# Attention, routed experts and a dense layer: masks and tails of two heads in one product, idle products in the drain, and where the low parts of the last routing are made

## The chip, the cores and the metric

One Trainium2 chip, one core. The metric is the time of one execution on the device in microseconds (us); lower is better. TensorE is called PE, its weight loads PEld, VectorE DVE, ScalarE ACT, GpSimd POOL, SyncE SP.

## The reference

Three layers, the output of each the input of the next, all in float32:

```python
# 1. attention: 4 batches x 8 heads, 576 tokens, head size 64
scores = q @ k.T / 8 ; bias = -(cum_i - cum_j), cum = cumsum(max(s, 0))
scores = where(j > i, -1e9, scores + minimum(bias, 0))
x = softmax(scores) @ v                       # as 2304 tokens x 512
# 2. experts: 8 experts of 512 -> 1024 -> 512, each token goes to one
e = argmax(x @ w_gate) ; g = softmax(x @ w_gate)[e]
x = g * (relu(x @ w1[e]) @ w2[e])
# 3. dense: 512 -> 2048 -> 512
h = relu(x @ w_in) ; out = (h * h) @ w_out
```

To keep float32 precision most operands are cut into a high part (a rounded copy, made by ACT) and a low part (what is left, a subtraction on DVE or POOL), and a product is made as high by high, high by low and low by high.

## The kernel before, in words

**Order of the work.** Attention and the first routing are not written in order. Each step is added to a planner (`Steps`, lines 31 to 150) with a key, the engines that may do it, a cost for each of them in ns, the steps it needs (`need`), the buffers it uses (`use`) and a due time. `Steps.run` (lines 67 to 150) is a list schedule made when the kernel is built: of the steps that could start within 60 ns of the earliest on an engine it takes the one due first, holding up to 200 ns (`HOLD`) for one due over 100000 ns (`URGENT`) earlier; due times are passed back to what a step needs (lines 68 to 70). Each engine then runs its instructions in that order, whatever they take on the chip. The experts and the dense layer (`Moe.run`, lines 1548 to 1631) are written out by hand.

**Attention** (lines 153 to 745). Work goes by head n = 0 to 31, in units of four heads; tails go by pairs. A sequence of 576 is four blocks of 128 and a tail of 64. `maxima` (521 to 608) makes a row maximum for the softmax: products into PSUM tiles `mx` (lines 536 and 539), DVE reductions (561, 581), and a DMA of the result back into the operand `qB` (607). `scores` (632 to 670) makes the scores transposed: `score` (622 to 630) is a product with `kA,qA` (626), one with `kB,qB` (627) and, on the diagonal, one with a mask (629). Each head has three pieces of 512 columns in tiles `tt` (piece 0 holds the four diagonal blocks), each pair one tail piece in tile `ot`: both heads' 64x64 corners, one on partitions 0 to 63, the other on 64 to 127. `expo` (672 to 688) takes a piece through exp on ACT (`P`, 679), a high part on ACT (`H`, 681) and a low part (`L`, 682) on POOL or DVE, as the planner likes. `pv` (690 to 745) multiplies with v (713): for the tail rows the 64x64 corners `H_t`, `L_t` use half of the array's rows. The result is scaled into `xb` (740 on DVE, 743 on ACT).

**Routing** (`gate`, 799 to 930) runs once a batch: transposes, logits (875), a chain of small DVE operations (906 to 927) with a product on PE in its middle (`rk`, 883 to 886), and POOL's indirect DMAs into the token table (894).

**The drain** (`Moe.first`, 1155 to 1326) is what lies between the last scores and the first expert product. It makes the first expert's input in four PSUM banks (`put_in`, 1217 to 1221, its products all have line 1220): tokens of earlier batches are gathered (1125), cut in high and low (`xgh` 1240, `xgl` 1242) and multiplied by unit blocks (`xgt`); those of the last batch are cut (`bh` 1268, `bl` 1272) and picked by 0/1 matrices `ones` (`at`, 1281; products `take`), which need the last routing's slots (926). Then ACT and DVE cut the banks (1299, 1302) and, after a branch (1450), the experts begin (1418 to 1420). PE, ACT, DVE and POOL have this in one queue each, in order.

The lines that the change touches, of those:

```python
self.mQt, self.mTt                                   # 64x64 masks, 249 to 250
for o in range(2): mm(ps[64*o:64*o+64, 0:64], h + o, 512, 64, 512, 64)   # t2, 555
if key[0] < self.NH - self.LDVE: ...                 # 685, LDVE = 32: never true
st.add(("xgl", c), {"Pool": 1120, "DVE": 600}, ..., due=soon)    # 1242
st.add(("bl", c), {"DVE": 800, "Pool": 1430}, low, ..., due=due) # 1277
```

Of the kernel before, what the change touches and what calls it, by code (L numbers as in the profile page):

```python
# [30 lines left out]
class Steps:  # L31
# [10 lines left out]
    URGENT = 100000  # L42

    def __init__(self, bufs):
        self.bufs, self.ops, self.by, self.users = bufs, [], {}, {}
        self.groups, self.after = [], {}
# [20 lines left out]
    def run(self):  # L67
        for op in reversed(self.ops):
            for p in op["need"]:
                p["due"] = min(p["due"], op["due"] - p["ns"] - 145)  # L70
        for op in self.ops:
            op["left"], op["next"] = len(op["need"]), []
# [31 lines left out]
        while ready:  # L104
# [15 lines left out]
            t, _, e, op = min(first, key=lambda x: x[:2])  # L120
            for u in op["use"]:
# [16 lines left out]
            ready.remove(op)  # L138
            for q in op["next"]:
# [13 lines left out]
class Attention:  # L153
# [86 lines left out]
    def setup(self, moe_constants):  # L240
# [8 lines left out]
        self.mQ, self.mQt = tile("mQ", [128, 128], BF16), tile("mQt", [64, 64], BF16)  # L249
        self.mT, self.mTt = tile("mT", [128, 128], BF16), tile("mTt", [64, 64], BF16)  # L250
# [24 lines left out]
        def mQ():  # L275
            nc.gpsimd.memset(self.mQ, 0.0)
            block(self.mQ, [[-1, 128]], 0, 1)
            nc.gpsimd.memset(self.mQt, 0.0)
            block(self.mQt, [[-1, 64]], 0, 1)
# [5 lines left out]
        def mTt():  # L285
            nc.gpsimd.memset(self.mTt, 0.0)
            block(self.mTt, [[1, 64]], 0, -1)
# [10 lines left out]

        self.gps("ident16", 560, lambda: nc.gpsimd.tensor_copy(out=self.ident16, in_=self.identb), need=["identb"])
# [221 lines left out]
    def maxima(self, n):  # L521
# [12 lines left out]
        def mm(out, h, i0, M, j0, N):  # L534
# [3 lines left out]
            if j0 + N > i0:  # L538
                nc.tensor.matmul(out=out[:, N - M:], lhsT=self.identb[0:M, 0:M], rhs=self.mQ if M == 128 else self.mQt,  # L539
                                 start=False, stop=True)  # L540
# [13 lines left out]
        def t2(ps):  # L554
            for o in range(2):
                mm(ps[64 * o:64 * o + 64, 0:64], h + o, 512, 64, 512, 64)

        def red(ps, *cols):

            for c, w, at, k in cols:  # L560
# [7 lines left out]
                 ("t2", 0, 240, t2, 70, ((0, 64, 17, 1),))]  # L568
# [53 lines left out]
    def score(self, u, ps, h, j0, M, i0, N, mask=False):  # L622
# [3 lines left out]
        nc.tensor.matmul(out=ps, lhsT=kA[:, j], rhs=qA[:, i], start=True, stop=False)  # L626
        nc.tensor.matmul(out=ps, lhsT=kB[:, j], rhs=qB[:, i], start=False, stop=not mask)  # L627
        if mask:
            nc.tensor.matmul(out=ps, lhsT=self.identb[0:M, 0:M], rhs=self.mT if N == 128 else self.mTt,  # L629
                             start=False, stop=True)  # L630

    def scores(self, n):
# [8 lines left out]
        def piece(p, ps):  # L641
            if p == 0:
# [1041 lines left out]
```

## Time and profile before

| | |
|---|---|
| median of 3 runs (lowest to highest) | 922.13 us (920.59 to 922.86) |
| the profiled execution, its own time | 922.22 us |
| its span in the trace | 920.7 us |
| busy: PE, PEld, DVE, ACT, POOL | 855.1, 728.7, 660.8, 494.9, 316.1 us |
| mean granted clock of TensorE | 0.967 |

A row of the timeline has the start, the duration, the engine, the line, the operation, what it writes and reads, the shapes and a count, and in brackets how long the engine was idle before and what ended that. Rows that lie close together are merged into one with a count. A PE duration holds the way through the array, so products overlap: what a product costs the stream is the distance from its start to the next start. The windows view has, for each stretch, its length, each engine's busy time with the number of instructions, the granted clock of TensorE (1.00 is 2.4 GHz, 0.50 is 1.2 GHz), the share of the DMA engines, and GB/s. Attention takes the first 230 us, the drain goes to 261 us, the experts to about 503 us, and the dense layer takes the rest.

### The profile page before, as it was taken

Reading aid. Unit: us, or ns where it says so; the run is one execution under the profiler, and the core shown is the slowest. Engines: PE = TensorE matmul, PEld = TensorE weight load, DVE = VectorE, ACT = ScalarE, POOL = GpSimd, SP = SyncE. Lnnn points to the kernel's source line nnn. Section 1 sums busy time; section 2 is a strip of 40 time slices with the busy share of each in tenths; the row PEclk is TensorE's granted clock in tenths of the full one; section 3 lists DMA queues with packets and bytes.
Section 4 is the critical chain, followed back from the end, with each engine's and each line's share of the span. In section 5 each row is a group of like instructions: output and inputs, shape, how many; then the busy total and the mean of one; then the engine's idle time right before and its main releaser. Section 6 shows DMA issues by size and latency. Waiting matters only on the chain.

```text
span 920.7 us, 17377 instructions
## 1 busy us (share of the span) xinstructions
PE 855.1 (93%) x6582; PEld 728.7 (79%) x6582; DVE 660.8 (72%) x1211; ACT 494.9 (54%) x1009; POOL 316.1 (34%) x356
## 2 busy tenths in 40 slices
PE   3889887889799999999999999999999999999995
PEld 2677665668689999998999777888888888888894
DVE  8699989888837798889889885554455445444673
ACT  3777776878434455545556444444454445444563
POOL 6667656756613355546433450020001001000100
PEclk9999997889679999999999999999999999999998
DMA  4886974980456666786664300010001000000100
GB/s 113 155 165 152 185 137 110 180 174 3 155 169 189 237 185 192 232 265 204 210 202 140 115 0 1 1 46 1 0 1 46 1 0 15 33 1 1 46 2 23
DMA packets 155489, 94.03 MB, mean 102 GB/s; under 512 B 115292, under 2 KB 140342, under 8 KB 155402
## 3 DMA queue, kind: packets, MB, share of 16 engines
q1 hardware_dynamic: 146766, 78.82, 32.7%
q0 software_dynamic: 4096, 10.19, 3.3%
q10 hardware_dynamic: 4540, 3.87, 1.4%
q8 instruction: 53, 0.87, 0.4%
q14 instruction: 34, 0.28, 0.1%
HBM read 70.16 MB, written 10.02 MB: 87 GB/s over the span
## 4 chain that ended last, share of the span: by engine, by line
PE 59%; issue 6%; DVE 5%; ACT 1%; POOL 0%; POOLq 0%; DVEq 0%; ACTq 0%
PE y_d L1500 7%; PE hd L1420 7%; PE hd L1419 7%; PE hd L1418 7%; PE y_d L1498 7%; PE y_d L1499 6%; PE y_e L1438 3%; PE y_e L1439 3%; PE y_e L1437 3%; PE he L1418 3%; PE he L1419 3%; PE he L1420 3%; DVE wae_6l L1348 1%; DVE wbe_6l L1348 1%; DVE wbe_7l L1348 1%
## 5 line engine op out<-in xcount | busy, mean ns | idle before, releaser
L1543 POOL DMA_INDIRECT out_dram<-o,ids x18 | 18.5, 1026 | 342.0 <-ACT o L1540 339.1
L1486 DVE TENSOR_TENSOR sqd<-hd,rld 128x512 f32<-128x512 f32 (+1 forms) x80 | 50.9, 637 | 112.5 <-ACT rld L1484 111.1
L1484 ACT ACTIVATE rld<-hd 128x512 f32<-128x512 f32 (+1 forms) x80 | 44.5, 556 | 130.5 <-PE hd L1420 130.5
L682 POOL TENSOR_TENSOR L<-P,H 128x512 f16<-128x512 f32 x58 | 71.0, 1231 | 59.1 <-ACT H L681 49.2
L1490 DVE TENSOR_TENSOR ald<-sqd,ahd 128x512 fp32r<-128x512 f32 (+1 forms) x80 | 51.1, 639 | 51.6 <-ACT ahd L1489 51.6
L1489 ACT CAST ahd<-sqd 128x512 fp32r<-128x512 f32 (+1 forms) x80 | 46.3, 579 | 74.1 <-DVE sqd L1486 74.1
L1400 POOL TENSOR_TENSOR lf<-lf,pw 128x512 f32<-128x512 f32 x32 | 50.0, 1564 | 74.6 <-DVE pw L1399 56.2
L713 PE MATMUL pv<-v,H 128*128 128x65 f16 (+1 forms) x896 | 59.1, 199 | 6.7 <-DVE xb L740 5.1
L679 ACT ACTIVATE P<-tt 128x512 f32<-128x512 f32 x96 | 55.3, 594 | 16.3 <-PE tt L629 8.8
L1427 ACT ACTIVATE hhe<-he 128x400 fp32r<-128x400 f32 (+7 forms) x64 | 27.9, 437 | 64.8 <-PE he L1420 60.9
L713 PE MATMUL pv<-v,L 128*128 128x65 f16 x448 | 54.8, 197 | 7.6 <-DVE L L682 7.6
L626 PE MATMUL tt<-qA,kA 128*128 128x128 f16 (+3 forms) x352 | 57.5, 232 | 3.8 <-ACT P L679 3.8
L627 PE MATMUL tt<-qB,kB 128*128 128x128 f16 (+3 forms) x352 | 60.7, 232 | 0.0
L713 PEld LDWEIGHTS <-H 128*128 128x128 f16 x896 | 48.5, 100 | 14.7 <-issue 7.3
L681 ACT CAST H<-P 128x512 f16<-128x512 f32 x96 | 57.0, 618 | 1.1 <-ACT P L679 1.0
L1125 POOL DMA_INDIRECT xg<-x_dram,idt x20 | 21.3, 1063 | 86.6 <-PE xps L1135 68.7
L713 PEld LDWEIGHTS <-L 128*128 128x128 f16 x448 | 43.9, 103 | 8.3 <-DVE L L682 8.1
L561 DVE TENSOR_REDUCE tops<-mxb 128x1 f32<-128x128 f32 (+2 forms) x96 | 43.6, 501 | 8.2 <-PE mxb L539 8.1
L682 DVE TENSOR_TENSOR L<-P,H 128x512 f16<-128x512 f32 x38 | 39.4, 1042 | 5.1 <-ACT H L681 4.4
L1428 DVE SCALAR_TENSOR_TENSOR hle<-he,hhe 128x400 fp32r<-128x400 f32 (+7 forms) x64 | 30.7, 480 | 16.7 <-ACT hhe L1427 16.4
L626 PEld LDWEIGHTS <-kA 128*128 128x128 f16 (+1 forms) x384 | 35.3, 102 | 7.9 <-issue 3.2
L627 PEld LDWEIGHTS <-kB 128*128 128x128 f16 (+1 forms) x384 | 34.4, 103 | 5.4 <-issue 4.1
(700 smaller groups left out, 3097.2 us busy)
## 6 DMA issues: line engine op xcount, KB each, us to landing
w0s<-in_moe_w_dram SPq DMA_DIRECT2D x30, 512.0 KB
w1s<-in_moe_w_dram SPq DMA_DIRECT2D x30, 512.0 KB
wout<-in_moe_w_in_dram SPq DMA_DIRECT2D x16, 512.0 KB
wout<-in_moe_w_out_dram SPq DMA_DIRECT2D x12, 512.0 KB
ldq<-in_q_dram SPq DMA_DIRECT2D x32, 128.0 KB
ldk<-in_k_dram SPq DMA_DIRECT2D x30, 128.0 KB
ldv<-in_v_dram SPq DMA_DIRECT2D x30, 128.0 KB
x_dram<-xb SPq DMA_DIRECT2D x3, 1024.0 KB
```

The lines of the kernel that those rows point to most:

```text
L626: nc.tensor.matmul(out=ps, lhsT=kA[:, j], rhs=qA[:, i], start=True, stop=False)
L627: nc.tensor.matmul(out=ps, lhsT=kB[:, j], rhs=qB[:, i], start=False, stop=not mask)
L679: self.act(("P",) + key, w, lambda: nc.scalar.activation(out=P(), in_=ps(), func=AF.Exp, scale=0.125), need=[T], use=[use, ("P", key), ("H ...
L681: self.st.add(("H",) + key, {"ACT": 0.833 * w + 80}, lambda: nc.scalar.copy(out=H(), in_=P()), need=[("P",) + key], use=[("P", key), ("H", ...
L682: f = lambda e="Pool": (nc.gpsimd if e == "Pool" else nc.vector).tensor_tensor(out=L(), in0=P(), in1=H(), op=ALU.subtract)
L713: nc.tensor.matmul(out=ps[0:M, I, 0:N], lhsT=a, rhs=m, start=(i == 0), stop=(i == len(ops) - 1))
L1418: nc.tensor.matmul(out=ps, lhsT=wh[:, k, :], rhs=xh[:, k, 0:C], start=(k == 0), stop=False)
L1419: nc.tensor.matmul(out=ps, lhsT=wh[:, k, :], rhs=xl[:, k, 0:C], start=False, stop=False)
L1420: nc.tensor.matmul(out=ps, lhsT=wl[:, k, :], rhs=xh[:, k, 0:C], start=False, stop=(k == 3))
L1498: nc.tensor.matmul(out=acc[t], lhsT=ah[:, c], rhs=wh, start=first, stop=False)
L1499: nc.tensor.matmul(out=acc[t], lhsT=ah[:, c], rhs=wl, start=False, stop=False)
L1500: nc.tensor.matmul(out=acc[t], lhsT=al[:, c], rhs=wh, start=False, stop=last)
```

## The change

1. **Masks**: the mask of the four diagonal blocks is one product of 512 columns, ahead of the eight score products, instead of four of 128 behind them.
2. **Tails**: the tail masks become 128x128 with two blocks; the tail of a pair is one 128x128 block whose off-diagonal quarters are masked, in `maxima` (t2, reduced over 128 columns instead of 64) and in `scores` (exp, high and low parts over 128 columns instead of 64). `pv` reads 128 rows of it.
3. **Low parts**: those of heads 30 and 31, all `xgl` and all `bl` (now in two steps) are on DVE alone.
4. **Idle products**: once the planner has placed the last score piece, and sees PE idle for over 250 ns, it puts in products of the identity with zeros for 0.8 of that gap: into unused columns of a `pv` bank in use, or into a free `o` or `mx` bank.

```diff
 # Steps
+    GAP = 250
+    PART = 0.8
 # in run(), where the next op is chosen; self.keep holds the score steps not yet placed
+            gap = t - free[e] if e == "PE" and self.fill and not any(self.keep) else 0
+            if gap > self.GAP:
+                tags, width, f, tag, w2, f2 = self.fill
+                live = [k for k in order.get(tag, [])[-2:] if left[k] > 2 and isinstance(k[1], int)]
+                i = int(self.PART * gap / w2)
+                if live and i:
+                    f2(*live[-1], i)
+                    tags = ()
+                for tag in tags:
+                    o, b = order.get(tag, []), self.bufs[tag]
+                    if len(o) >= b and not left[o[-b]]:
+                        s = max(free[e], freed[o[-b]])
+                        i = int(self.PART * (t - s) / width)
+                        if i > 0:
+                            k = (tag, ("fill", n))
+                            f(*k, i)
...
 # setup
-            block(self.mQt, [[-1, 64]], 0, 1)
+            block(self.mQt, [[-1, 128]], 0, 1)
+            block(self.mQt[64:128], [[1, 128]], -64, 0)
...
-            block(self.mTt, [[1, 64]], 0, -1)
+            block(self.mTt, [[1, 128]], 0, -1)
+            block(self.mTt[0:64], [[-1, 128]], 63, 0)
+        def fill(tag, key, n):
+            out = self.tile(tag, key, [128, 512], F32)[:, 0:256]
+            for _ in range(n):
+                nc.tensor.matmul(out=out, lhsT=self.identb, rhs=self.mrow.bitcast(BF16)[:, 0:256], start=True, stop=True)
+        def fill_pv(tag, key, n):
+            for _ in range(n):
+                nc.tensor.matmul(out=self.tile(tag, key)[:, 328:512], lhsT=self.identb,
+                                 rhs=self.mrow.bitcast(BF16)[:, 0:184], start=True, stop=True)
+        self.st.fill = ("o", "mx"), 110, fill, "pv", 80, fill_pv
 # maxima
         def t2(ps):
-            for o in range(2):
-                mm(ps[64 * o:64 * o + 64, 0:64], h + o, 512, 64, 512, 64)
+            mm(ps[:, 0:128], h, 512, 128, 512, 128)
...
-                 ("t2", 0, 240, t2, 70, ((0, 64, 17, 1),))]
+                 ("t2", 0, 256, t2, 128, ((0, 128, 17, 1),))]
 # scores
             if p == 0:
+                self.nc.tensor.matmul(out=ps, lhsT=self.identb, rhs=self.mT.unsqueeze(1).to_broadcast([128, 4, 128]),
+                                      start=True, stop=False)
                 for J in range(4):
-                    self.score(u, ps[:, 128 * J:128 * J + 128], h, 128 * J, 128, 128 * J, 128, True)
+                    self.score(u, ps[:, 128 * J:128 * J + 128], h, 128 * J, 128, 128 * J, 128, on=True, more=J < 3)
...
-                for o in range(2):
-                    self.score(u, ps()[64 * o:64 * o + 64, :], h + o, 512, 64, 512, 64, True)
+                self.score(u, ps(), h, 512, 128, 512, 128, True)
...
-            self.expo((n, "t"), 64, ps, ("o", ("t", n)))
+            self.expo((n, "t"), 128, ps, ("o", ("t", n)))
 # expo
-        if key[0] < self.NH - self.LDVE:
+        if key[0] > self.NH - 3:
+            self.dve(("L",) + key, 1.04 * w, lambda: f("DVE"), **kw)
+        elif key[0] < self.NH - self.LDVE:
 # pv
-                    key, c = (n - n % 2, "t"), 0
-                    r, M = slice(64 * (h % 2), 64 * (h % 2) + 64), 64
-                    v = vt()[r, blk + 8, :]
+                    key, c = (n - n % 2, "t"), 64 * (h % 2)
+                    r, M, v = slice(0, 128), 128 - c, vt()[:, blk + 8, :]
 # Moe.first
-            st.add(("xgl", c), {"Pool": 1120, "DVE": 600}, lambda e, ...
-                use=[ug] + u, due=soon)
+            at.dve(("xgl", c), 560, lambda ...
+                use=[ug] + u, due=due)
...
-            st.add(("bl", c), {"DVE": 800, "Pool": 1430}, low, need=[("bh", c)], ..., due=due)
+            for i, n in ((0, 560), (1, 170)):
+                at.dve(("bl", c, i), n, lambda i=i, low=low: low(i), need=[("bh", c)], ..., due=due)
```

## Rows read from the trace of the kernel before

**Rows 1.** Windows: attention after its start, its end, the drain in two parts.

```profile
40.00:232.00 192.00, 165.93 (x2754) 131.63 (x2753) 170.63 (x396) 148.65 (x360) 128.10 (x143) 0.93 0.68 137
...
200.00:230.00 30.00, 29.18 (x577) 24.75 (x574) 24.85 (x69) 24.90 (x62) 19.03 (x24) 1.00 0.14 22
230.00:246.00 16.00, 10.49 (x134) 8.78 (x135) 14.31 (x37) 9.35 (x30) 10.80 (x12) 0.79 0.27 78
246.00:256.00 10.00, 10.00 (x60) 9.86 (x57) 5.68 (x28) 1.23 (x2) 5.91 (x10) 0.50 0.73 239
```

**Rows 2.** Waits of DVE for PE, 40 to 232 us: first and last of seven (total, times, longest).

```profile
DVE tops L561 <- PE mxb L539: 4.7, 5, 1.8
...
DVE g_s L889 <- PE ork L886: 0.3, 1, 0.3
```

**Rows 3.** Timeline of PE: one pair's tail scores, then the tail maxima.

```profile
110.58 0.22 PE L626 MATMUL ot<-qA,kA 128*64 128x64 f16 x1
...
111.22 0.43 PE L536 MATMUL mxt<-kB,qB 128*64 128x512 f16 x3
111.59 0.21 PE L539 MATMUL mxt<-mQt,identb 64*64 64x64 bf16 x1
...
112.02 0.23 PE L626 MATMUL tt<-qA,kA 128*128 128x128 f16 x1
```

**Rows 4.** Timeline of PE: the tail corner within one head's `pv`.

```profile
104.98 0.19 PE L713 MATMUL pv<-v,L 128*128 128x65 f16 x1
105.10 0.25 PE L713 MATMUL pv<-v,H_t 64*64 64x65 f16 x2
...
105.31 0.24 PE L713 MATMUL pv<-v,H 128*128 128x65 f16 x2
```

**Rows 5.** Groups by line and shape: the tail's reduction (busy us, mean ns, idle before).

```profile
L561 DVE TENSOR_REDUCE tops<-mxt 128x1 f32<-128x64 f32 x16 | 3.5, 216 | 2.5 <-PE mxt L539 2.2
```

**Rows 6.** Groups by line and shape: a tail mask's making, before 40 us.

```profile
L268 POOL TENSOR_SCALAR_AFFINE_SELECT mQt<-mQt 64x64 bf16<-64x64 bf16 x1 | 0.3, 332 | 0.1
```

**Rows 7.** Timeline of the drain: PE at the last pair's tail.

```profile
231.01 0.21 PE L713 MATMUL pv<-v,L_t 64*64 64x65 f16 x1 [1.44 <-POOL L_t L682]
```

**Rows 8.** Timeline of the drain: DVE, from a last low part to the 0/1 matrices.

```profile
228.62 2.17 DVE L682 TENSOR_TENSOR L<-P,H 128x512 f16<-128x512 f32 x1 [0.57 <-ACT H L681]
...
239.65 1.35 DVE L1272 TENSOR_TENSOR hlb<-xb,hhb 64x128 fp32r<-64x128 f32 x1
...
242.05 1.14 DVE L909 TENSOR_TENSOR g_sel<-g_lg,g_mx 128x40 f32<-128x40 f32 x1
...
244.41 1.26 DVE L914 TENSOR_TENSOR g_oh<-g_sel,g_smx 128x40 bf16<-128x40 f32 x1
...
247.31 1.40 DVE L1281 TENSOR_SCALAR Pones<-xbg,g_slot 128x256 fp32r<-128x256 f32 x5
```

**Rows 9.** Timeline of the drain: POOL, one of its last low parts.

```profile
239.33 1.52 POOL L1272 TENSOR_TENSOR xlb<-xb,xhb 128x512 fp32r<-128x512 f32 x1 [0.47 <-ACT xhb L1268]
```

**Rows 10.** Timeline of the drain: PE, products of line 1220 and the first expert product.

```profile
242.15 0.28 PE L1220 MATMUL pvacc<-s4aux,alx 128*128 128x128 f32 x1
242.26 0.27 PE L1220 MATMUL pvacc<-s4aux,ahx 128*128 128x128 f32 x1
...
250.77 0.41 PE L1220 MATMUL ttacc<-Pones,xlb 128*128 128x256 f32 x1
250.98 0.41 PE L1220 MATMUL ttacc<-Pones,xhb 128*128 128x256 f32 x1
...
259.04 0.28 PE L1220 MATMUL pvacc<-Pones,hlb 64*128 64x256 f32 x1
261.29 0.67 PE L1418 MATMUL he<-xhf,ahw 128*128 128x400 f32 x1 [1.98 <-DVEq L1450]
```

**Rows 11.** Timeline of PE: idle products at the kernel's start.

```profile
22.88 1.37 PE L295 MATMUL oidle<-mrow,identb 128*128 128x256 bf16 x11
```

**Rows 12.** Low parts of line 682 on DVE: ns min/median/max, first and last start.

```profile
L682 DVE TENSOR_TENSOR L<-P,H x38: 643/688/6493, 32.8 to 228.6; 128x512 f16<-128x512 f32 x38
```

More of the change, by code (lines that the diff above doesn't have):

```diff
@@ L42 @@
     URGENT = 100000
+    GAP = 250
+    PART = 0.8
     def __init__(self, bufs):
-        self.bufs, self.ops, self.by, self.users = bufs, [], {}, {}
-        self.groups, self.after = [], {}
+        self.bufs, self.ops, self.by, self.users, self.fill = bufs, [], {}, {}, None
+        self.groups, self.after, self.keep = [], {}, []
     def group(self, old, new, f):
@@ L70, in run @@
                 p["due"] = min(p["due"], op["due"] - p["ns"] - 145)
+        self.keep = [op["key"] for op in self.ops if op["key"][0] == "T"]
         for op in self.ops:
@@ L138, in run @@
             ready.remove(op)
+            if op["key"][0] == "T":
+                self.keep.pop()
             for q in op["next"]:
@@ L538, in mm @@
             if j0 + N > i0:
-                nc.tensor.matmul(out=out[:, N - M:], lhsT=self.identb[0:M, 0:M], rhs=self.mQ if M == 128 else self.mQt,
-                                 start=False, stop=True)
+                nc.tensor.matmul(out=out[:, N - M:], lhsT=self.identb, rhs=self.mQt if i0 == 512 else self.mQ, start=False, stop=True)
         def b1(o, ps):
@@ L620, in seg, with score @@
         return (2, 128 * I - 128) if J == 1 else (2, 384)
-    def score(self, u, ps, h, j0, M, i0, N, mask=False):
+    def score(self, u, ps, h, j0, M, i0, N, mask=False, on=False, more=False):
         nc = self.nc
@@ L625, in score @@
         j, i = self.cols(h, j0, M), self.cols(h, i0, N)
-        nc.tensor.matmul(out=ps, lhsT=kA[:, j], rhs=qA[:, i], start=True, stop=False)
-        nc.tensor.matmul(out=ps, lhsT=kB[:, j], rhs=qB[:, i], start=False, stop=not mask)
+        nc.tensor.matmul(out=ps, lhsT=kA[:, j], rhs=qA[:, i], start=not on, stop=False)
+        nc.tensor.matmul(out=ps, lhsT=kB[:, j], rhs=qB[:, i], start=False, stop=not (mask or more))
         if mask:
-            nc.tensor.matmul(out=ps, lhsT=self.identb[0:M, 0:M], rhs=self.mT if N == 128 else self.mTt,
-                             start=False, stop=True)
+            nc.tensor.matmul(out=ps, lhsT=self.identb, rhs=self.mTt if i0 == 512 else self.mT, start=False, stop=True)
     def scores(self, n):
@@ L1268, in high, with low @@
                     nc.scalar.copy(out=o, in_=i)
-            def low(e, rows=rows, src=src):
-                for o, i, h in zip(rows("l"), src(), rows("h")):
-                    (V if e == "DVE" else nc.gpsimd).tensor_tensor(out=o, in0=i, in1=h.bitcast(F32), op=ALU.subtract)
+            def low(i, rows=rows, src=src):
+                V.tensor_tensor(out=rows("l")[i], in0=src()[i], in1=rows("h")[i].bitcast(F32), op=ALU.subtract)
             norms = [("norm", at.H * b + 2 * c + i) for i in range(2)]
@@ L1276, in first @@
             at.act(("bh", c), 780, high, need=norms, use=ub)
-            st.add(("bl", c), {"DVE": 800, "Pool": 1430}, low, need=[("bh", c)], use=ub + [("xl", "b"), ("hl", "b")], due=due)
+            for i, n in ((0, 560), (1, 170)):
+                at.dve(("bl", c, i), n, lambda i=i, low=low: low(i), need=[("bh", c)], use=ub + [("xl", "b"), ("hl", "b")], due=due)
         ones = lambda t: at.tile("P", ("ones", t), [128, 512], F32R)[:, LO:C]
@@ L1290, in first @@
         ub = [(x + y, "b") for x in "xh" for y in "hl"]
-        bl = [("bl", c) for c in range(4)]
+        bl = [("bl", c, i) for c in range(4) for i in range(2)]
         for t in range(3):
```

11 lines of the change are left out of this document (7 added, 4 removed).

## The prediction

> **What bounds the kernel now.** I read the windows first, in stretches cut where the work changes, then the waits, then the timelines of PE and DVE. The change touches only attention and the drain; experts and dense layer keep their instructions and start when the drain ends, so what is won before 261 us is won at the end.
>
> In attention no engine stands out alone [rows 1]: of the 192 us from 40 to 232, DVE is busy 170.6 and PE 165.9. They wait for each other: seven rows of DVE's waits name PE, 13.0 us in all [rows 2]. Only at its end, from 200 to 230 us, is PE clearly the bound (29.2 of 30 us, DVE 24.9) [rows 1]. So faster products pay in full there, and earlier at most by DVE's waits.
>
> In the drain the bound changes hands. From 230 to 246 us DVE is busy 14.3 of 16 us and PE 10.5; from 246 to 256 us PE is busy throughout, at a granted clock of 0.50, that is 1.2 GHz [rows 1]. PE had been idle for a third of the stretch before. The first expert product starts at 261.29 [rows 10].
>
> **Attention, step by step.**
> *Masks.* Four products of 128 columns become one of 512: the same number of columns, so I take 0. What could be won or lost is the weight loads' part, which PEld's 131.6 us against PE's 165.9 [rows 1] says is hidden.
> *Tails in the scores.* Six small products of a pair run from 110.58 to 111.22, 0.64 us [rows 3]. Three full ones of 128 columns replace them; idle products of 256 columns take 1.37 us for eleven [rows 11], so I estimate 0.06 for 128 columns, 0.18 for the three: 0.46 us saved.
> *Tails in the maxima.* The last three of four products run from 111.59 to 112.02, 0.43 us [rows 3]; two of 128 columns take 0.12: 0.31 saved.
> *Tails in pv.* From the start of the last full product, 104.98, to that of the next, 105.31, it takes 0.33 us for one full product and three corners [rows 4]. Four full ones of 65 columns at 0.03 each (half of the 0.06, by columns) take 0.12: 0.21 a head, 0.42 a pair.
> Together 1.2 us a pair, 19 us of PE's stream over 16 pairs.
> *What grows.* The tail's reduction has twice the columns: 16 of 216 ns now [rows 5], so at most 3.5 us more on DVE and, as part of an operation is fixed, I take 1. ACT's and POOL's tail pieces grow in the same way and hide, ACT being busy 149 and POOL 128 of 192 us [rows 1]. Three more mask instructions on POOL at the start, about 0.3 each [rows 6], stand ahead of its low parts of the first q and k; PE then waits for operands anyway, so 0, and 1 if not.
>
> How much of 19 us is on the path? At the end, where PE is the bound, two and a half pairs give 3 us. Before that the gain is at least nothing (DVE stays the bound, and pays 1 us more) and at most DVE's 13 us of waits. PE and DVE are within 5 us of each other, so as PE gets faster DVE soon is late next. I take half of the waits less DVE's 1 us, **6 us in all**, with ends of 0 and 13.
>
> **The drain, step by step.**
> *Last tail.* PE waited 1.44 us for a low part on POOL [rows 7], while DVE's own took 2.17 us [rows 8] where the median is 0.69 [rows 12]. On DVE alone the three of them take about 0.69 + 0.69 + 0.3 and end at 230.3 rather than 231.0: 0.7 us. Queued behind them on DVE are the scaling steps of head 30, which pv waits for next; they move with it.
> *Clock.* From 230 to 246 the mean is 0.79 over 10.5 us of PE's work [rows 1]: at 1.00 the work is 2.2 us shorter, half of which (the last head's pv) is on the path: 1.1 us.
> *Stretched steps.* Three DVE operations take 1.35, 1.14 and 1.26 us [rows 8], the first within POOL's subtraction from 239.33 to 240.85 [rows 9]. Operations of that size take about 0.28 (a 0/1 matrix, 1.40 for five [rows 8]): 2.9 us of stretch that goes when POOL has no low part left. In exchange DVE takes over POOL's four (two of `bl`, two of `xgl`), about 0.69 + 0.28 + 0.69 + 0.69, 2.3 us. The due time given to `xgl` changes nothing, since `xgt` keeps its early due time and hands it back; `xgl` still goes between the routing's small steps. Net 0.6 us. On POOL the last routing's five table writes stood behind these low parts and come sooner; the next expert's token list waits for them, and that is off the path to the first product.
> So DVE has the 0/1 matrices and all low parts done at 248.7 - 0.7 - 1.1 - 0.6 = 246.3.
> *Products.* Forty `take` products follow. The first 24 cost 0.21 us each at the lower clock [rows 10]; at the full clock products of line 1220 stand 0.11 apart [rows 10]. The last 16 change between 128 and 64 rows and take about 0.21 each as it is, the clock being full by then. Now they begin at about 250.4, because PE is still at products delayed by the clock. After: 246.3, 0.9 for a last block of eight, 24 x 0.11 = 2.7, 16 x 0.215 = 3.5: PE's last product ends near 253.4, against 259.3 now, **6 us** earlier. The planner's remaining steps on DVE (expert order, weight splits, some 3.6 us) lie beside these 6 us of products. The wait for the branch behind it, 1.98 us [rows 10], stays, and so does the low clock of the first expert step.
> If the clock stays low all the same: 246.3 + 1.1 (the clock term falls away) + 1.7 + 5.0 + 3.5 = 257.6, 2 us gained. These are the ends of this term: 2 and 7.
> *Idle products.* They cost the path nothing if the gap that the planner sees is there on the chip: eleven in 1.37 us, 0.12 each [rows 11], against 110 ns planned. Those in `o` and `mx` banks wait for the last reader of the bank, and real products stand behind them in PE's queue; 0.8 of the gap is the margin.
>
> **Sum.** 6 + 6 = 12 us. The profiled execution took 922.22 us, the median of the three runs is 922.13, so no correction is due: 922.2 - 12 = **910 us**.
>
> **Rivals.**
> *PE was not the limit.* Attention keeps its length because DVE paces it; only the drain gains: 922 - 6 = 916. For it: DVE busy 170.6 of 192. Against it: 13 us of waits for PE.
> *The clock stays low.* The idle products are too few or wait for banks, the drain gains 2: 914. For it: the planner's gaps are not the chip's. Against: PE's idle share is plain there.
> *All of it.* DVE's waits for PE go entirely, 13 + 7: 902.
> *The other side: idle products overrun.* The planner counts 110 ns for each; at the lower clock 256 columns take 0.21 [rows 10]. The stretch from 230 to 246 has 5.5 us without PE work [rows 1]; the planner, not knowing the late starts, may see 8. Then 0.8 x 8 / 0.11 = 58 products take 12.2 us in a queue with 5.5 us of room: PE's real work comes 6.7 us later, and the low parts gain nothing. 922 + 6.7 = 929 without a gain in attention, 923 with the forecast one. It decides where the clock falls before the idle products come, and attention gains under 4.
> *Small products ran side by side.* The pair's tail products take 0.64 us for 64 columns each, one after the other, and slower than full ones [rows 3]. The Trainium skill (TensorEngine Tiling (Array Packing), Key Properties) says that different tiles of the array load and multiply in parallel, by which joining two heads would give up a twofold use; no such overlap is seen in these rows. As a mechanism: if tail corners cost 0.03 us each in pairs, the change would lengthen PE's stream by about 0.1 a pair, attention would gain nothing and lose 2, and the drain's 6 leave 918.
>
> **Chances.** Forecast (906 to 914, the clock rival beside it at 914): 0.45 and 0.10. PE not the limit, 916: 0.18. All of it, 902: 0.15. Overrun, 923 to 929: 0.08. Side by side, 918: 0.02. The remaining 0.02: a new plan with other collisions; one low part on DVE took 6.49 us where 0.69 is the median [rows 12], and any change of the plan can make or undo such a one, of 5.8 us. This blurs every case by some 4 us. A measurement here can tell about 0.3% (2.8 us) from no change: faster is below 919.4. Of the 916 case a quarter lies above that by the blur, of the forecast a twentieth. Faster 0.82, same 0.09, slower 0.09. The range leaves out about 0.08 below and 0.12 above: 899 to 920.
>
> **What would show it.** Right: `ot` and `mxt` rows only of 128x128 and one pair's tail under 0.2 us; PE's busy time from 40 us to the last score down by some 15 us and DVE's waits for PE about halved; the last scores some 6 us earlier; a granted clock near 1.00 from 230 us to the last `take`; no DVE row of the drain stretched over 1 us; no low part on POOL there; the first expert product near 249 us and from there the same length as before, 659 us. Wrong: idle products that stand between a ready product and PE; DVE's busy time in attention unchanged with PE idle in its place; a new row of several us at line 682; an expert stage that is longer than before.

## The result, and the profile after

The changed kernel takes 913.93 us (median of 4 runs, 911.95 to 914.25) where the kernel before took 922.50 beside it (4 runs, 920.59 to 923.86): ratio 0.9904, 95% interval 0.9881 to 0.9927, 8.6 us faster, where 12 were forecast. The profiled execution took 913.95 us with a span of 912.4 (before: 922.22 and 920.7).

Three points cut the span into the stages of the forecast: the last score product, the first expert product, the end.

| | before | after | forecast |
|---|---|---|---|
| last score product starts | 226.64 | 222.69 (-3.95) | -6 |
| from there to the first expert product | 34.65 | 29.43 (-5.2) | -6 |
| from there to the end of the span | 659.4 | 660.3 (+0.9) | 0 |

**Attention.** The window of the kernel after that answers to the first of [rows 1] (length, then busy us of PE, PEld, DVE, ACT, POOL, the granted clock, DMA share, GB/s):

```profile
40.00:232.00 192.00, 157.73 (x2696) 124.58 (x2694) 178.56 (x412) 151.98 (x366) 134.01 (x138) 0.94 0.71 140
```

PE and DVE were within 5 us of each other; now PE has 157.7 us of work in the 192 and DVE 178.6. (The same window holds some 4 us more of the drain than before; up to the last score, PE fell from 162.2 to 149.4 and DVE rose from 165.8 to 170.2.) What the two engines wait for has turned round as well. First all waits of DVE for PE from 40 to 232 us (total, times, longest), then the longest group of PE's waits from 40 to 222 us:

```profile
DVE sums L772 <- PE pv L753: 2.0, 2, 1.4
DVE tops L599 <- PE mxt L575: 1.6, 2, 1.0
DVE tops L599 <- PE mxb L578: 1.3, 2, 1.1
DVE tops L619 <- PE mxb L578: 1.0, 2, 0.9
```

```profile
PE mxrow L637 <- DVE twice L634: 10.0, 8, 3.3
```

DVE's 13.0 us of waits for PE [rows 2] are 5.9, and PE now waits 10.0 us for `twice` alone, a step of 18 columns.

The small products went as forecast but for one. A pair's tail scores, then its tail maxima, in the timeline of PE of the kernel after (against [rows 3]):

```profile
109.58 0.22 PE L664 MATMUL ot<-qA,kA 128*128 128x128 f16 x1
...
109.75 0.22 PE L575 MATMUL mxt<-kB,qB 128*128 128x128 f16 x1
...
109.86 0.23 PE L753 MATMUL pv<-v,H 128*128 128x65 f16 x2
```

Three score products take 0.17 us (before 0.64, forecast 0.18), two of the maxima 0.11 (before 0.43 for three of the four, forecast 0.12). The tail within `pv` is another matter. From the last full product ahead of the corner to the first one behind it, in the same timeline, a pair's even head and then its odd head:

```profile
113.19 0.19 PE L753 MATMUL pv<-v,L 128*128 128x65 f16 x1
...
113.31 0.22 PE L753 MATMUL pv<-v,H 128*128 128x65 f16 x2
...
117.19 0.19 PE L753 MATMUL pv<-v,L 128*128 128x65 f16 x1
117.31 0.25 PE L753 MATMUL pv<-v,H_t 128*64 128x65 f16 x2
...
117.52 0.24 PE L753 MATMUL pv<-v,H 128*128 128x65 f16 x2
```

The even head takes 0.12 us, as forecast. The odd head takes 0.33, as before [rows 4]: its `M` is `128 - c`, 64, so its weights are 128 by 64, and the change of shape costs what it cost. That a change of shape has such a price shows in the tail scores of the kernel before, behind the first row of [rows 3]:

```profile
110.63 0.20 PE L627 MATMUL ot<-qB,kB 128*64 128x64 f16 x1
110.76 0.21 PE L629 MATMUL ot<-mTt,identb 64*64 64x64 bf16 x1
```

Two products of one shape start 0.05 us apart (110.58 and 110.63), the next, of another shape, 0.13 us later, and the one behind it, of the first shape again, another 0.14. The stream is shorter by 0.47 + 0.32 + 0.21 = 1.0 us a pair, not 1.2.

**The drain.** PE between the routing's ranks and the first expert product, kernel after:

```profile
239.37 3.81 PE L330 MATMUL ofill<-mrow,identb 128*128 128x256 bf16 x17 [0.49 <-DVE base L930]
242.83 0.56 PE L1260 MATMUL ttacc<-Pones,xhb 128*128 128x256 f32 x1
...
249.51 0.28 PE L1260 MATMUL pvacc<-Pones,hlb 64*128 64x256 f32 x1
252.12 0.67 PE L1458 MATMUL he<-xhf,ahw 128*128 128x400 f32 x1 [2.33 <-ACT wbe_1h L1387]
```

Seventeen idle products, planned at 17 x 0.11 = 1.9 us, take about 3.5 (from their start to the next product's). The first 0/1 matrix is done at about 241.45 on DVE (five from 241.17, 0.28 the first), so the first `take` came 1.4 us late for want of PE. Why 0.2 each is in the windows of PE (busy us, granted clock, DMA share, GB/s):

```profile
226.00:230.00 4.00, 3.93 (x80) 1.00 0.16 45
230.00:234.00 4.00, 3.70 (x58) 1.00 0.51 162
234.00:238.00 4.00, 3.77 (x38) 0.92 0.61 181
238.00:242.00 4.00, 3.45 (x34) 0.50 0.96 346
242.00:246.00 4.00, 4.00 (x27) 0.73 0.91 287
...
250.00:254.00 4.00, 1.88 (x6) 0.63 0.60 143
```

The clock was at 0.50 from about 237.4 to 244.2 us, although PE had been busy for 11.4 of the 12 us before. So the last 19 of the drain's 47 idle products and the first six of the forty `take` products ran at the lower of the two levels, 1.2 GHz, and the clock fell once more behind the last `take`.

### The profile page after: what moved, and what is told of

It reads as the page before. It is cut to its first block, busy times and chain, and to the rows that moved or that the text cites. A ratio compares the mean times of both kernels' runs of the same rounds, so it can differ in the third digit from the quotient of the medians.

```text
span 912.4 us, 17097 instructions
## 1 busy us (share of the span) xinstructions
PE 840.4 (92%) x6453; PEld 715.1 (78%) x6453; DVE 665.0 (73%) x1217; ACT 492.5 (54%) x1002; POOL 315.6 (35%) x347
## 4 chain that ended last, share of the span: by engine, by line
PE 58%; DVE 7%; issue 6%; ACT 1%; POOL 0%; DVEq 0%; POOLq 0%; ACTq 0%
PE y_d L1540 7%; PE y_d L1538 6%; PE hd L1460 6%; PE y_d L1539 6%; PE hd L1459 6%; PE hd L1458 6%; PE y_e L1478 3%; PE y_e L1479 3%; PE y_e L1477 3%; PE he L1458 3%; PE he L1459 3%; PE he L1460 3%; DVE wae_6l L1388 1%; DVE wbe_6l L1388 1%; DVE wbe_7l L1388 1%
## 5 line engine op out<-in xcount | busy, mean ns | idle before, releaser
L1583 POOL DMA_INDIRECT out_dram<-o,ids x18 | 18.5, 1026 | 342.0 <-ACT o L1580 339.1
L720 POOL TENSOR_TENSOR L<-P,H 128x512 f16<-128x512 f32 x56 | 73.7, 1327 | 35.9 <-ACT H L719 26.3
L665 PE MATMUL tt<-qB,kB 128*128 128x128 f16 (+3 forms) x352 | 55.1, 232 | 0.3 <-DMA qB<-ms 0.3
L664 PE MATMUL tt<-qA,kA 128*128 128x128 f16 (+3 forms) x352 | 51.2, 232 | 4.0 <-ACT P L717 3.8
L665 PEld LDWEIGHTS <-kB 128*128 128x128 f16 x368 | 32.3, 101 | 12.0 <-issue 6.8
L575 PE MATMUL mxb<-kB,qB 128*128 128x128 f16 (+3 forms) x128 | 32.0, 319 | 9.9 <-DVE qB L500 6.0
L664 PEld LDWEIGHTS <-kA 128*128 128x128 f16 x368 | 33.5, 101 | 5.8 <-issue 2.4
```

The source lines that it names most:

```text
L720: f = lambda e="Pool": (nc.gpsimd if e == "Pool" else nc.vector).tensor_tensor(out=L(), in0=P(), in1=H(), op=ALU.subtract)
```

## The experiments

Twelve kernels, each timed in five rounds beside the kernel before; each diff is against the kernel that it edits, which is the changed one where nothing else is said. First the four parts are taken out one at a time, then two are put alone into the kernel before; then the idle products are varied; then the two engines are charged. The stages of each, in us, from the timelines of PE:

| kernel | last score | to first expert product | rest of span | ratio to before (95%) |
|---|---|---|---|---|
| before | 226.6 | 34.7 | 659.4 | 1 |
| after | 222.7 | 29.4 | 660.3 | 0.9904 (0.9881, 0.9927) |
| e1, no idle products | 224.2 | 30.1 | 657.8 | 0.9902 (0.9882, 0.9922) |
| e2, no joined tails | 228.1 | 33.1 | 659.0 | 0.9959 (0.9944, 0.9975) |
| e3, low parts shared | 225.6 | 32.8 | 659.6 | 0.9948 (0.9929, 0.9967) |
| e4, four masks | 222.1 | 29.0 | 660.3 | 0.9902 (0.9885, 0.9919) |
| e5, before + tails | 222.3 | 33.7 | 660.0 | 0.9929 (0.9904, 0.9953) |
| e6, before + low parts | 224.9 | 32.6 | 658.2 | 0.9974 (0.9956, 0.9992) |
| e7, idle behind `take` | 220.8 | 32.3 | 657.7 | 0.9890 (0.9871, 0.9909) |
| e8, fewer idle | 220.7 | 28.2 | 659.2 | 0.9909 (0.9893, 0.9926) |

Read the second column with care: after, e1, e7 and e8 give PE and the other engines the same instructions in the same order up to the last score (idle products come only behind it), and their last scores lie between 220.7 and 224.2. A difference of 2 us in one profile's attention says nothing. The drain is steadier.

**e1: without idle products.**

```diff
-            if gap > self.GAP:
...
-        self.st.fill = ("o", "mx"), 110, fill, "pv", 80, fill_pv
```

> The changed kernel without its idle products (nothing fills the gaps that the planner sees); all else as changed. My theory: they hold the clock up behind 237 us for part of the drain only, and are worth about 3 us: ratio to before near 0.994 (some 917 us against 914), the last scores within 0.5 us of 222.7, the first `take` earlier than 242.8 since no idle product stands in front of it, but the granted clock low from some point after 237 us to the end of the `take` products and the first expert product 2 to 4 us later than 252.1. Rival: the seventeen idle products in front of the first `take` cost as much as the clock gives back: ratio 0.990 or less, first expert product at 252 us or before.

The rival is right: 0.9902 against 0.9904. Windows of PE in e1, with the first and the last `take` and the first expert products:

```profile
226.00:230.00 4.00, 2.89 (x53) 0.73 0.09 6
230.00:234.00 4.00, 4.00 (x43) 0.50 0.55 167
...
242.00:246.00 4.00, 2.62 (x12) 0.50 1.01 332
```

```profile
243.38 0.58 PE L1224 MATMUL ttacc<-Pones,xhb 128*128 128x256 f32 x1 [2.77 <-DVE Pones L1285]
...
251.65 0.28 PE L1224 MATMUL pvacc<-Pones,hlb 64*128 64x256 f32 x1
254.34 0.42 PE L1422 MATMUL he<-xhf,ahw 128*128 128x400 f32 x1 [2.42 <-ACT wbe_1h L1351]
```

Without idle products the clock is low from about 228 to 235 us, which delays the last head, and again in the first half of the `take` products, which take 8.3 us instead of 6.7. Against that the first `take` starts 0.1 us behind its operand, not 1.4. The drain is 0.7 us longer in all, and the first expert products start at the full clock (0.18 us apart, 0.34 in the kernel after): the 25th of them comes 8.2 us behind the first, in the kernel after 9.2, which gives 1.0 us back. So the idle products do move the clock, and are worth nothing here that the times show (the two intervals leave some 3 us).

**e2: tails of 64 again.** Masks, low parts and idle products stay.

```diff
-                 ("t2", 0, 256, t2, 128, ((0, 128, 17, 1),))]
+                 ("t2", 0, 240, t2, 70, ((0, 64, 17, 1),))]
...
-                self.score(u, ps(), h, 512, 128, 512, 128, True)
+                for o in range(2):
+                    self.score(u, ps()[64 * o:64 * o + 64, :], h + o, 512, 64, 512, 64, True)
```

> The changed kernel with the tails of two heads as two blocks of 64 again, in scores, maxima and pv; masks, low parts and idle products as changed. My theory: the shorter PE stream is what gave the 4 us in attention: ratio near 0.995 (918 us), last scores near 226 us, PE busy before the last score up by some 14 us, DVE's waits for PE back at 10 us or more. Rival: VectorE is the bound and the 4 us came from the new plan and the moved low parts: ratio 0.990, last scores within 1 us of 222.7.

0.9959: 5 us of the 8.6 are gone. PE is busy 162.1 us from 40 us to the last score (after 149.4), and DVE's waits for PE from 40 to 232 us come to 13.5 us; the longest group:

```profile
DVE tops L597 <- PE mxb L575: 6.1, 7, 2.7
```

My theory held in attention. The 3.7 us in the drain were not expected. By the timelines 2.2 of them lie ahead of the first 0/1 matrix (20.7 us behind the last score, 18.5 in the kernel after; e6 shows a part of it), 1.1 in idle products (the first `take` starts 2.5 us behind its 0/1 matrix, not 1.4) and 0.7 in the `take` products (7.4 us, not 6.7), less 0.3 in the wait behind them.

**e3: low parts shared again.**

```diff
-        if key[0] > self.NH - 3:
-            self.dve(("L",) + key, 1.04 * w, lambda: f("DVE"), **kw)
-        elif key[0] < self.NH - self.LDVE:
+        if key[0] < self.NH - self.LDVE:
...
-            at.dve(("xgl", c), 560, ...
+            st.add(("xgl", c), {"Pool": 1120, "DVE": 600}, ...
...
+            st.add(("bl", c), {"DVE": 800, "Pool": 1430}, low, ...
```

> The changed kernel with its low parts beside the last routing shared between VectorE and GpSimd again, as before; tails, masks and idle products as changed. My theory: GpSimd's low parts stretch VectorE's steps again, so one to three VectorE rows of the drain take over 1 us, and the drain from the last score to the first expert product is 2 to 3 us longer (32 us instead of 29.4): ratio near 0.993. Rival: moving them changes only who does the work: the drain stays within 1 us of 29.4, ratio 0.990.

0.9948, a drain of 32.8 us against 29.4: as my theory said. The rows of DVE in its drain that show it:

```profile
226.20 1.12 DVE L1246 TENSOR_SCALAR xbg<-xbg,leadf 128x4 f32<-128x4 f32 x1 [1.21 <-POOL xbg L1240]
...
234.82 1.95 DVE L1310 TENSOR_TENSOR xlb<-xb,xhb 128x512 fp32r<-128x512 f32 x1
...
241.95 1.31 DVE L954 TENSOR_TENSOR g_d<-g_lg,g_mx 128x40 f32<-128x40 f32 x1
```

The first of them works on four elements a partition and takes 0.23 us in the kernel after.

**e4: four masks again.**

```diff
-                self.nc.tensor.matmul(out=ps, lhsT=self.identb, rhs=self.mT.unsqueeze(1).to_broadcast([128, 4, 128]), ...
...
-                    self.score(u, ps[:, 128 * J:128 * J + 128], h, 128 * J, 128, 128 * J, 128, on=True, more=J < 3)
+                    self.score(u, ps[:, 128 * J:128 * J + 128], h, 128 * J, 128, 128 * J, 128, True)
```

> The changed kernel with one mask product of 128 columns for each of the four diagonal blocks again; all else as changed. My theory: equal columns, so no change: ratio 0.990, within 0.002, last scores within 1 us of 222.7. Rival: each product has a fixed part of about 0.03 us, three fewer in each of 32 heads are worth up to 3 us of PE's stream: ratio 0.992 to 0.993.

0.9902 and 0.9904: nothing. PE is busy 149.0 and 149.4 us up to the last score, and the weight loads that fall away (PEld 121.6 against 117.4) were beside products.

**e5: the kernel before with joined tails.** The parts of the change's diff for `mQt`, `mTt`, `t2`, `tail` and `pv`, nothing else.

> The kernel before with the tails of two heads as one block in scores, maxima and pv, and nothing else. My theory: attention gains all that the changed kernel gained there: last scores within 1.5 us of 222.7 (before: 226.6), VectorE's waits for TensorE from 40 us on near 6 us instead of 13, and the drain stays near 34.7 us: ratio 0.995 to 0.996 (918 us). Rival: the shorter products pay only together with the moved low parts: last scores at 225 us or later, ratio 0.998 to 1.

0.9929, and a profile with last scores at 222.3: the attention gain is the tails' alone, my theory. The time gained more than I had expected, 6.6 us for some 4. The drain stays at 33.7, with five stretched steps of DVE:

```profile
222.92 1.11 DVE L1208 TENSOR_SCALAR xbg<-xbg,leadf 128x4 f32<-128x4 f32 x1 [1.22 <-POOL xbg L1202]
...
224.34 2.35 DVE L1211 TENSOR_SCALAR s4aux<-ident,xbg 128x128 fp32r<-128x128 f32 x4
...
232.62 2.05 DVE L1272 TENSOR_TENSOR hlb<-xb,hhb 64x128 fp32r<-64x128 f32 x1
...
236.79 1.78 DVE L1272 TENSOR_TENSOR xlb<-xb,xhb 128x512 fp32r<-128x512 f32 x1
238.49 1.35 DVE L1272 TENSOR_TENSOR hlb<-xb,hhb 64x128 fp32r<-64x128 f32 x1
```

8.6 us in all, for work that takes 2.4 unstretched (0.23 and 0.96 for the first two in the kernel after; 0.27, 0.68 and 0.27 for the others where e5 has such a row unstretched).

**e6: the kernel before with the low parts on DVE.**

```diff
+        if key[0] > self.NH - 3:
+            self.dve(("L",) + key, 1.04 * w, lambda: f("DVE"), **kw)
...
-            st.add(("xgl", c), {"Pool": 1120, "DVE": 600}, ...
+            at.dve(("xgl", c), 560, ...
...
-            st.add(("bl", c), {"DVE": 800, "Pool": 1430}, low, ...
+            for i, n in ((0, 560), (1, 170)):
+                at.dve(("bl", c, i), n, ...
```

> The kernel before with the low parts beside the last routing on VectorE alone, and nothing else. My theory: no change before the last scores (226.6, within 1.5), and a drain shorter by 2 to 3 us, 32 to 33 us from the last score to the first expert product: ratio 0.997 (919.5 us). Rival: what VectorE takes over (four low parts, 2.3 us) costs as much as the stretched rows: drain 34 us or more, ratio 1.000. Second rival: the whole gain of 5 us seen when the low parts were shared again is in this part alone: ratio 0.995.

0.9974 and a drain of 32.6: my theory, 2.1 us. Behind joined tails the same edit gave 3.6 us (33.7 in e5, 30.1 in e1, which differ beside it in the masks alone, and those are worth nothing). The reason is read from a row of ACT and one of DVE in e6's drain; the second stands between the routing's small steps:

```profile
240.65 0.62 ACT L1242 CAST bhx<-xbg 128x512 fp32r<-128x512 f32 x1 [2.06 <-DMA xbg<-x_dram,idtf]
...
241.31 0.69 DVE L1244 TENSOR_TENSOR blx<-xbg,bhx 128x512 fp32r<-128x512 f32 x1 [1.64 <-ACT bhx L1242]
```

`xgl` stands in DVE's queue ahead of the rest of the routing and waits 1.64 us, by way of ACT, for a gathered tile that is late; the routing waits behind it. That is about what the gain is short of 3.6 us. In e2 the same wait is 1.04 us, in the kernel after 0.57, and there ahead of the routing's small steps; in e1 there is none.

**e7: idle products behind the last `take`.** The one idle stretch that the change left in front of a low clock.

```diff
+        at.pe("warm", 18 * 256, lambda: [nc.tensor.matmul(
+            out=at.tile("o", "warm", [128, 512], F32)[:, 0:256], lhsT=at.identb, rhs=at.mrow.bitcast(BF16)[:, 0:256],
+            start=True, stop=True) for _ in range(18)], need=[("take", 3, 3)], use=[("o", "warm")])
```

> The changed kernel with 18 more idle products of 256 columns behind the last `take`, where TensorE stood idle for 2.33 us before the first expert product. My theory: they take 2.0 us there, the granted clock stays at 1.00 beyond 251.3 us, the first expert step runs at the full clock, and the kernel is 2 to 2.5 us faster than the changed one: ratio 0.988. Rival: the clock falls all the same, or the idle products stand in front of the expert product: first expert product later than 252.5 us, ratio 0.990 to 0.993.

The timeline of PE in e7, from the last `take` to the first expert products:

```profile
248.03 0.27 PE L1260 MATMUL pvacc<-Pones,hlb 64*128 64x256 f32 x1
248.23 2.14 PE L1346 MATMUL owarm<-mrow,identb 128*128 128x256 bf16 x18
253.08 0.42 PE L1462 MATMUL he<-xhf,ahw 128*128 128x400 f32 x1 [2.72 <-PEq L1494]
253.35 0.34 PE L1463 MATMUL he<-xlf,ahw 128*128 128x400 f32 x1
253.53 0.35 PE L1464 MATMUL he<-xhf,alw 128*128 128x400 f32 x1
```

Both halves of theory and rival came true. The clock stays up, the expert products are 0.18 us apart, and the rest of the span is 2.6 us shorter (657.7). But the first of them comes 4.8 us behind the last `take`, not 2.3: PE waits 2.72 us at its branch once its own queue is empty, so that what stands in front of the branch is added to it. 0.9890 can't be told from 0.9904.

**e8: idle products planned at their low price.**

```diff
-        self.st.fill = ("o", "mx"), 110, fill, "pv", 80, fill_pv
+        self.st.fill = ("o", "mx"), 220, fill, "pv", 80, fill_pv
```

> The changed kernel with an idle product in an o or mx bank planned at 220 ns, as it takes at the lower clock, instead of 110: half as many, 8 instead of 17 in front of the first `take`. My theory: the first `take` no longer stands behind idle products but starts within 0.2 us of its last operand, 1 to 1.4 us earlier relative to the last score; the clock rises no later than now (6.5 us after its fall): ratio 0.989. Rival: with fewer the clock rises later, the `take` products run at the lower clock longer and the gain is given back: ratio 0.990 to 0.991, `take` products over 7.5 us in all instead of 7.0.

The timeline of PE in e8:

```profile
237.18 1.89 PE L330 MATMUL ofill<-mrow,identb 128*128 128x256 bf16 x8 [0.49 <-DVE base L930]
...
239.37 0.58 PE L1260 MATMUL ttacc<-Pones,xhb 128*128 128x256 f32 x1 [0.31 <-DVE Pones L1321]
```

Of the profile my theory is right: the first `take` starts 0.1 us behind its first 0/1 matrix (from 238.98, 0.28 us), and the drain is 28.2 us, the shortest of all, 1.3 less than after. The forty `take` products take 7.2 us instead of 6.7, part of the gain given back as the rival said. Of the time it can't be told: 0.9909.

**e9 to e12: which engine sets attention's pace.** Each kernel is charged with more work for one engine, the planner's costs and the order of the work unchanged: 10.3 us for PE, and for DVE what was planned as 10 us. These ran on a chip on which the kernel before took 927.67 us (21 runs), so they are compared by ratio alone. The changed kernel without a dose was not run there; its 0.9904 is carried over. Each of their profiles has in attention a wait of 3.0 to 5.4 us that something outside the core ends (the view of waits calls it `remote`); no other profile here has one.

```diff
         def t1(ps):
+            for _ in range(6):
+                nc.tensor.matmul(out=ps[:, 0:256], lhsT=self.identb, rhs=self.mrow.bitcast(BF16)[:, 0:256], start=True, stop=True)
```

```diff
-        ... ("t1", 0, 520, t1, 520, ((0, 512, 8, 1),)),
+        ... ("t1", 0, 520, t1, 520, ((0, 256, 8, 1), (0, 256, 8, 1), (0, 512, 8, 1))),
```

> The changed kernel with six idle products of 256 columns (0.107 us each) ahead of each pair's tail maxima, 16 pairs, 10.3 us more for TensorE in attention; the planner's costs and so the order of the work are those of the changed kernel. My theory: after the change VectorE is the bound and TensorE has room, so the time grows by a third of the dose, about 3 us: ratio to before 0.993 to 0.995. Rival: TensorE still sets the pace, the dose shows in full: ratio 1.000 to 1.002.

> The changed kernel with two more reductions of 256 columns (about 0.33 us each) ahead of each pair's tail reduction, 16 pairs, about 10 us more for VectorE in attention; same order of the work. My theory: VectorE is now the bound and 8 us or more of the dose show: ratio to before 0.998 to 1.002. Rival: both engines have room, because they wait for each other in turn: 3 to 5 us, ratio 0.994 to 0.996.

> The kernel before with the same dose for TensorE, 10.3 us. My theory: before the change the two engines were level, so a microsecond of TensorE is worth more here than behind the change: 5 to 8 us, ratio to before 1.005 to 1.009. Rival: VectorE was the bound already, and the dose is worth a third here too: 3 us, ratio 1.003.

> The kernel before with the same dose for VectorE, about 10 us. My theory: level engines, so 5 to 8 us: ratio to before 1.005 to 1.009, less than the same dose costs behind the change. Rival: VectorE was the bound already: 9 us or more, ratio 1.010 or more, as much as behind the change.

DVE's dose is larger than planned. All of it in e10, by line and shape (busy us, mean ns):

```profile
L599 DVE TENSOR_REDUCE tops<-mxt 128x1 f32<-128x256 f32 x32 | 13.4, 418 | 0.9 <-PE mxt L575 0.3
```

In e10's timeline a pair's two extra reductions and its two own take 1.79 us, where in the kernel after its own two take 0.88 in one row: 0.91 us a pair, 14.5 us for 16, and as much in e12.

| | ratio to before (95%) | the dose shows as | share of the dose |
|---|---|---|---|
| e11, before, PE + 10.3 us | 1.0110 (1.0079, 1.0141) | 10.2 us | 0.99 |
| e12, before, DVE + 14.5 us | 1.0078 (1.0050, 1.0106) | 7.2 us | 0.50 |
| e9, after, PE + 10.3 us | 0.9941 (0.9921, 0.9961) | 3.4 us | 0.33 |
| e10, after, DVE + 14.5 us | 1.0005 (0.9986, 1.0024) | 9.4 us | 0.65 |

(The third column is the ratio's distance from 1, or from 0.9904 for the changed kernel, times 927.67; each is good to some 3 us.) Behind the change both ratios are where my theory had them, though a third of DVE's dose does not show. Before it, e12's ratio is where I had it, for a larger dose, and e11's is above both theories, its interval reaching down into mine. So before the change a microsecond of PE cost about a full one and one of DVE about half; behind it PE's costs about a third and DVE's some two thirds. In e9 and e10 the dose is not the only thing that moved: the longest `twice`, 3.08 us in the kernel after, is 1.12 and 1.13 there, so the order in time changed by some 2 us in their favour, and both shares are rather lower bounds.

## Why the prediction was right, and where its steps were not

**The sum.** 910 was forecast and 913.9 came, within the range; faster was given 0.82. By the profiles, of what is missing 2 us are in attention, 0.8 in the drain and 0.9 behind it. By the times, the tails alone are worth 6.6 us (e5) and the low parts alone 2.4 (e6), together 9.0, where the whole change has 8.9 by its ratio; taken out, the tails cost 5.1 us (e2) and the low parts 4.1 (e3). So these two parts make the gain. How it splits between them, and between attention and the drain, is known to 2 or 3 us.

**Attention, the mechanism.** Right as far as it is shown: PE's stream shrinks in the tails, masks cost nothing, DVE waits less for PE, the gain is a fraction of the stream. e5 has all of it with the tails alone, and e2 loses it without them. Over ten profiles, joined tails put the last score at 222.6 us on the mean (seven kernels, 220.7 to 225.6), separate ones at 226.5 (three, 224.9 to 228.1): 3.9 us, though the two ranges touch.

How much of this the shorter stream brings is not shown, because joined tails also change the plan. The low part of 6.49 us on DVE [rows 12] is there in all three profiles with separate tails (6.49, 6.54 and 6.56 us in the kernel before, e2 and e6), beside a chain of POOL's subtractions for k and q, and PE waits for it. From the timeline of PE of the kernel before:

```profile
154.13 0.24 PE L713 MATMUL pv<-v,L 128*128 128x65 f16 x1 [5.29 <-DVE L L682]
```

In all seven profiles with joined tails this row is gone, and another DVE step, `twice`, meets the same chain (see the next paragraph); PE then waits 2.8 to 4.0 us. The difference, 1.3 to 2.5 us, is a third to two thirds of the 3.9. The prediction named such a row under its chances, not as a term. No run holds the plan and shortens the products alone.

**Attention, the size.** "I take half of the waits less DVE's 1 us" failed in its second half. The waits did fall by half, 7.1 us of 13.0. But DVE grew by 4.4 us up to the last score, not by 1. The tail's reduction grew by 0.9 as forecast (4.4 us for 16 where [rows 5] had 3.5). The rest is the sum of larger changes, from 40 us to the last score: the tail's low parts on DVE, which the forecast had only as pieces of ACT and POOL that hide, went from 1.1 us (4 of 64 columns) to 5.8 (8 of 128), `twice` from 3.7 to 9.6, and the long low parts from 34.6 to 25.7. That is a new plan with other collisions. `twice`, first before and then after (16 each; ns min, median, max):

```profile
L596 DVE TENSOR_TENSOR twice<-tops x16: 164/174/1130, 22.1 to 215.5; 128x18 f32<-128x18 f32 x16
```

```profile
L634 DVE TENSOR_TENSOR twice<-tops x16: 164/288/3084, 21.9 to 212.3; 128x18 f32<-128x18 f32 x16
```

The longest of them, with POOL's rows beside it and the PE product that waited, from the timeline of the kernel after:

```profile
145.78 2.26 POOL L453 TENSOR_TENSOR hlq<-ldq,hlq 128x512 f16<-128x512 f32 x2
...
146.87 3.08 DVE L634 TENSOR_TENSOR twice<-tops 128x18 f32<-128x18 f32 x1
...
148.01 0.41 POOL L453 TENSOR_TENSOR hlk<-tlk,hlk 128x128 f16<-128x128 f32 x1
148.39 0.41 POOL L453 TENSOR_TENSOR hlq<-tlq,hlq 128x128 f16<-128x128 f32 x1
148.78 1.14 POOL L720 TENSOR_TENSOR L<-P,H 128x512 f16<-128x512 f32 x1
...
150.10 0.59 PE L637 MATMUL mxrow<-eighth,twice 128*18 128x128 f32 x2 [2.84 <-DVE twice L634]
```

POOL works without a gap until 149.92, and a step of 18 columns, 0.17 us by itself, ends at 149.95. The longest `twice` is 4.24, 3.45, 3.45, 4.19, 3.62 and 3.11 us in e1, e3, e4, e5, e7 and e8, all with joined tails; in e2 and e6, with separate ones, it is 1.13. The Trainium skill (SBUF — State Buffer, SBUF: two separate sides) says that a VectorE operation with two inputs in SBUF and a GpSimd operation that reads SBUF share a pair of ports, which one of them holds for a whole instruction. The trace agrees with the stretch and shows more of it: the VectorE step did not get the pair in any of the changes from one GpSimd instruction to the next.

So the rival "PE was not the limit" was wrong of the kernel before (e11: PE's dose shows in full), and is nearer to right of the kernel after (e9: a third of it shows). I read from this that the first microseconds taken from PE pay, and that then DVE is late; the doses added work and took none away, so how much the first ones pay was not run.

**Masks.** 0, as forecast (e4).

**The `pv` corner.** The forecast took full products for both heads; the odd head's stay 64 wide and cost what they did. 0.21 us a pair instead of 0.42.

**The drain, its terms.** The total was nearly right, 5.2 for 6, by luck: the terms were not. Forecast: low parts 1.3 us (last tail 0.7, stretched steps 0.6), the rest from the clock. Measured: joined tails alone 0.9 (34.7 to 33.7, e5), low parts 3.6 (33.7 to 30.1, e1), idle products 0.7 (30.1 to 29.4). The clock's term was 4 us too large, the low parts' 2.3 too small, and the 0.9 was not forecast. The step "2.9 us of stretch that goes" was mis-sized: it counted three late rows of one profile, and e5 shows five rows with 6.2 us of stretch, of which the drain got 3.6 back. "No DVE row of the drain stretched over 1 us" held, as did "no low part on POOL there".

**The clock.** "A granted clock near 1.00 from 230 us to the last `take`" was wrong. The idle products removed the first low stretch (in e1 it is there from 228 to 235 us, in the kernel after not), but the clock fell at 237.4 all the same. The rival with idle products that overrun came true in small: 1.4 us in front of the first `take`, where it had put 6.7. It had 58 of them in one stretch; the planner put 47 into the whole drain, 17 of them in front of the first `take`. e8 takes the overrun out.

**Behind the drain.** The wait at the branch stayed, 2.33 us for 1.98, and so did the low clock of the first expert step, as forecast. That the rest of the span is not quite constant (657.7 to 660.3) was not. In e7 it is this step's clock: the 25th expert product starts 6.7 us behind the first, in the kernel after 9.2. In e1 that makes 1.0 of 2.5 us. For the other differences no cause is shown.

**Small products side by side.** The joined block was faster by 0.47 us in scores and 0.32 in maxima, and e2 with separate tails is slower. The Trainium skill (TensorEngine Tiling (Array Packing), Key Properties) says that different tiles of the array work in parallel; no trace here shows that of these products, which start one after the other, 0.05 to 0.14 us apart [rows 3].

**What stays open.** How the 4 us in attention divide between PE's shorter stream and the collision that went was not run, and ACT and POOL were not charged. Whether `xgl` with its new due time would stand elsewhere was not run. No version was clearly better than the changed kernel: e7 and e8 each shorten a stage of the profile by 1.3 to 2.6 us, and are level with it in time.

## What to carry to other kernels

Before making one engine's stream shorter, ask what a microsecond of it is worth, by a dose put on each engine in turn, and read the size of the dose from its trace: here PE's was worth about all of it, and 13 us less of PE still brought only 4, with DVE level with it and a new plan that moved DVE's steps into and out of POOL's chains. Work that shares a port is worth more on one engine alone than its own duration says: count the stretched rows of every step around it, over more than one profile. Filler work that was priced at the full clock overran at the lower one by 1.4 us, and ahead of a branch it added its own length to the wait; the times could tell neither.

## What was not expected of the hardware

- The clock fell to 0.50 at 237.4 us after 12 us in which PE's records show it busy for 11.4. The last of its work were eight products with 16 rows and 16 columns, 0.11 us apart, from 236.49 us on. PE's busy time in the profile did not tell that the clock would fall.
- The wait ahead of the first expert product, behind PE's branch, is 1.6 to 2.8 us in all ten profiles of the table, and as long behind 18 idle products (2.72, e7) as without: there it began with PE's last product, not with the data.
- A VectorE step of 18 columns was held 3.08 us beside a chain of short GpSimd instructions, each of at most 1.2 us: not one of the changes between them let it in.
- The same order of instructions in attention ended between 220.7 and 224.2 us in four profiles.
